# A new order of one step's instructions in a fused convolution, gelu and two-matrix kernel

## The chip, the cores and the metric

The kernel runs on one core of a Trainium2 chip. Its time is the device time of one execution in microseconds (us). A core has a matrix engine (TensorE, PE in the profile, with its weight loads listed as PEld), a vector engine (VectorE, DVE), an activation engine (ScalarE, ACT), a general engine (GpSimd, POOL) and an engine that here only issues transfers (SyncE, SP). Each engine works through its own instructions in the order in which they were written, and waits where one needs something that isn't there yet. SBUF is the memory on the chip that all engines read and write; PSUM is the small memory in eight banks that TensorE writes its products to.

## The reference

The input x is 8 sequences of 4096 rows of 192 values. Each of 8 heads (24 columns each) has 7 weights; after a softmax over the 7, every column is convolved along its sequence with its head's weights, looking back only:

```
w   = exp(weight - max) / (sum + 1e-9)                   # 8 x 7
out[b, s, h, :] = sum over k of w[h, k] * x_pad[b, s + k, h, :]      # 7 taps, 6 zeros in front
```

The result, as 32768 rows of 192, goes through two matrices with a gelu between them:

```
h = x @ w_in                          # 192 -> 2048
g = h * (1 / (1 + exp(-1.702 * h)))
return g @ w_out                      # 2048 -> 192
```

All of it is float32 (w_in and w_out come as float64 and are brought to float32 in the kernel's opening).

## The kernel before, in words

**Steps.** The rows are cut into 32 steps (`big` = 0 to 31); a step takes 512 rows from a sequence of the first four and the same 512 from its counterpart in the other four. Steps 0 and 1 have a prologue and a list of their own (`OPENING`) for their first products; steps 2 to 31 run through `first_products(big, ..., ORDER)`. Steps 1 to 31 then run `second(...)` with the list `PLAN`. Nothing is planned at run time or by a scheduler: `ORDER` and `PLAN` are lists written by hand, and the position of an item in its list is the position of its instructions on the engine that carries them out. Two items on different engines can change places in the list without a change to either engine's order; two items on one engine can't.

**First products, x @ w_in.** Both matrix products are done with fewer multiplications than the plain way, in the manner of Strassen: sums of blocks of the left matrix times sums of blocks of the right one, and the products added and subtracted into the results. For x @ w_in there are 20 block products (`TERMS`) for each half of the columns, so 40 in a step. A product is four matmul passes of 64 rows by 512 columns (L598 in the profile): two row halves of TensorE work side by side on two banks, and each matmul counts as two passes. A pair of passes, one for each row half, is the unit of the rhythm; a product has two pairs.

An item of `ORDER` has this form: the half that it belongs to (0, 1, or 2 for the next step's half 0), its kind and its operands. Operands whose name begins with `a` are pairs of PSUM banks, taken from a list of free ones at the first use and given back after the last one (so the order also decides which banks a product gets); those that begin with `k` are rooms in SBUF (`ROOM_OF` says which, and several names share one room).

- `(v, "prod", t, "aN")`: product t is added into aN (TensorE, L598).
- `(v, "copy", "kN", "aM", 1)`: ScalarE copies PSUM to a room (L633), or, with -1, negates in PSUM (L635). The copy of a product into a room is what later products of the other half, or of the same, are taken from.
- `(v, "sum", d, a, op, b)`: VectorE adds or subtracts (L639), each 128x512 half apart where a PSUM bank is in it.
- `(v, "gelu", b, u, src, sign)`: ScalarE's gelu of a finished block of h, written to `g` (L615 from PSUM, L620 from a room). Gelus k9 and k7 are those of the rooms with these names.
- `("tap",)`: ScalarE multiplies x of the step after next by one weight of the convolution (L483). `("add", n)`: POOL adds n such taps to the convolution's blocks `conv_t` (L501); the last columns' taps are added by accumulating DMAs instead (`tree`, L506).
- `("done",)`: what is left of the taps' additions for the next step, one more sum of blocks on POOL, and the crossing of that "open" block. `("begin",)` puts the next step's ten sums of blocks (`SUMS_C`) on a list, and every `("vsum",)` carries out one on POOL (L355 and L357, `conv_t<-conv_t`). `("cross",)` issues the two transfers on SP's queue that copy finished blocks to the other row half (L526), where the matmuls of that row half read them.
- `("turn", c)`: VectorE transposes one third of x (L438). `("turn", 2)` is the last reader of the buffer `xin`, and issues the loads of x for the step after (eight transfers on SP's queue, L78).
- `("g", i)`: entry i of `EARLY_G`, a sum of blocks of `g` that the second products need (VectorE, L355 and L357; blocks 0 and 1 are in `osbs`). Entry 0 makes block 6, entry 1 makes block 0 in `osbs`, entry 2 adds that block into block 8 by an accumulating DMA that POOL issues (L831, `g<-osbs`), entries 3 and 4 make block 1.

At the end of the first products of half 0 the items of half 1 are already mixed in, and at the end of half 1 the next step's product 0 and (in `final` of `PLAN`) its copy k8.

**Second products, g @ w_out.** `PLAN` has 25 products of 128 rows by 32 columns in four column tiles (L855): three of the tiles work on the "main" product, the fourth on a "side" product. `("main", f, s, to, first)` and `("side", f, s, to)` name them, and each `("go", n)` issues n groups of four column tiles; there are 78 groups. A finished side product is copied out of PSUM by ScalarE (L880). `("seed", d, s, sign)` is a copy on ScalarE that starts a bank or a room from another, `("join", d, a, op, b)` a sum of such values on VectorE (L357, 96x256), `("sum", d, a, op, b)` a sum of blocks of `g` on VectorE (L357, 128x1024), and `("acc", d, a)` one by an accumulating DMA of POOL's queue. `turn` and `store` transpose the result on VectorE and send it out on SP's queue; `tap`, `tree`, `vsum` and `cross` are those from above, for the steps to come.

**What follows what around the change.** In half 0, the room that the sum k0 reads (as k8) is the room that the copy k4 writes, and k4 frees bank a3 for product 14. Product 2 writes a3, product 6 writes a8, which k0 reads. At the end of half 1 stand the sums a7 and k7 on VectorE: the last product (before: 13) waits for a7, and the second products' banks come free with k7 and the copies and gelus after it. Product 19 of either half writes bank a4, which the negated copy a5 reads just before.

Of the kernel before, what the change touches and what calls it, by code (L numbers as in the profile page):

```python
# [15 lines left out]
def kernel(  # L16
# [80 lines left out]
    g = consts.tile([P, NG, 2, 2, NG, T], F32)  # L97
# [398 lines left out]
    tree, adds = [], []  # L496
# [144 lines left out]
    def plain(u, m, n, v, slot, ks=range(NC), first=0):  # L641
# [2 lines left out]
            product1(slot, NC * (2 * u + m) + k, 2 * k + n, 0, v, k == first)  # L644

    ORDER = [
        (0, "prod", 6, "a8"), (0, "sum", "k0", "a8", "-", "k8"), (0, "prod", 2, "a3"), (0, "copy", "k4", "a3", 1),
        (0, "prod", 12, "a2"), ("tap",), ("tap",), ("tap",), ("tap",), ("add", 4), (0, "prod", 16, "a0"),
# [4 lines left out]
        (0, "prod", 10, "a4"), ("turn", 1), (0, "gelu", 3, 1, "k3", 1), (0, "prod", 17, "a1"),  # L653
# [6 lines left out]
        ("turn", 2), (1, "copy", "k4", "a3", 1), (0, "gelu", 3, 0, "k9", 1), (1, "prod", 12, "a2"), ("done",),  # L660
        ("begin",), ("vsum",), (1, "prod", 16, "a0"), (1, "sum", "a1", "a2", "-", "k0"), (1, "prod", 14, "a3"),
        (1, "copy", "k1", "a0", 1), ("g", 0), (1, "prod", 9, "a2"), (1, "sum", "a4", "a2", "-", "k1"),
        (1, "prod", 3, "a1"), ("vsum",), ("vsum",), ("vsum",), ("vsum",), (1, "copy", "k2", "a1", 1),
        (1, "prod", 15, "a3"), (1, "prod", 7, "a4"), ("vsum",), (1, "prod", 1, "a1"),
# [3 lines left out]
        (1, "prod", 19, "a4"), (1, "prod", 11, "a1"), ("vsum",), (1, "prod", 8, "a5"),  # L668
        (1, "sum", "a6", "k6", "-", "a4"), (1, "prod", 5, "a4"), (1, "gelu", 0, 1, "a1", 1), ("g", 4),
        (2, "prod", 0, "a3"), (1, "gelu", 1, 0, "a5", 1), (1, "sum", "a7", "a4", "+", "k2"),  # L670
        (1, "gelu", 2, 1, "k5", 1), (1, "prod", 4, "a6"), (1, "prod", 13, "a4"), ("vsum",),
        (1, "sum", "k7", "a7", "-", "k6"), (1, "sum", "k9", "a4", "-", "k0"), (1, "gelu", 0, 0, "a6", 1),
        (1, "gelu", 2, 0, "k7", 1), ("cross",), (1, "gelu", 3, 0, "k9", 1), ("cross",), ("done",),
    ]
    SEED_AHEAD = ("copy", "k8", "a3", 1)
    ROOM_OF = ((4, 0, 3, 2, 1, 1, 0, 1, 1, 2), (0, 1, 4, 2, 3, 3, 2, 3, 3, 2))
# [97 lines left out]
    def store(big, n, o=None, queues=(nc.sync,) * 3):  # L774
# [13 lines left out]
        (6, 6, "-", 10), (0, 5, "+", 6), (8, 8, "+", 0), (1, 7, "-", 6), (1, 1, "-", 11),  # L788
    ]
    PLAN = [  # L790
        ("side", 13, 16, "k0"), ("main", 1, 5, "p2", 1), ("vsum",), ("go", 2), ("sum", 14, 14, "-", 18), ("go", 1),
        ("vsum",), ("vsum",), ("go", 1), ("main", 16, 10, "p3", 0), ("go", 1), ("tap",), ("go", 1), ("vsum",),
        ("go", 2), ("main", 0, 14, "p0", 1), ("go", 2), ("seed", "p4", "p2", 1), ("go", 1), ("seed", "k1", "p3", 1),
# [34 lines left out]
    def sum_g(dst, a, op, b=None):  # L828

        if op == "acc":  # L830
            nc.gpsimd.dma_start(out=spot(dst), in_=spot(a), accum_op=ALU.add)  # L831
        else:
            add_up(spot, dst, a, op, b)
# [3 lines left out]
    def second(big, bx, bs, by, final, last):  # L837
# [5 lines left out]
        side, count = [], [0]  # L843
# [47 lines left out]
        def out_store(n, o):  # L891
# [9 lines left out]
            sum=sum_g, acc=lambda d, a: sum_g(d, a, "acc"), main=begin_main, side=begin_side, go=go, seed=seed,  # L901
            join=lambda d, a, op, b: add_up(value, d, a, op, b), turn=out_turn, store=out_store,
            tap=next_tap, cross=cross_piece, final=final, vsum=next_sum, tree=add_taps,
        )
        for item in PLAN:
            ops[item[0]](*item[1:])
        assert not side and not now["steps"] and count[0] == NC * len(SIDE_HALF)
        while sums_left:
# [355 lines left out]
```

## Time and profile before

| | |
|---|---|
| median of 3 runs | 2262.8 us (2262.54 to 2262.89) |
| profiled execution | 2262.78 us, of which its span is 2261.1 us |
| PE busy | 2248.2 us, 99% |
| VectorE busy | 1985.3 us, 88% |
| ScalarE busy | 1707.7 us, 76% |
| POOL busy | 1063.9 us, 47% |
| PE, L598 (first products, steps from 1) | 5152 matmuls of 64x512 |
| transfers, mean over the span | 132 GB/s |
| q0, the queue that POOL's transfers run on | 150.69 MB, 37.0% of 16 engines' span |
| q1, the one that SP's run on | 142.99 MB, 27.8% |
| granted TensorE clock | 1.00 |

Busy time of PE is modelled from the starts, so 99% tells that it rarely has nothing in flight, not that it never loses time. In a row of the timeline stand, from left to right, the start in us from the span's beginning, the time from the first start to the last end, the engine, the line, the operation, what it writes and reads, the shape, and how many instructions of that kind the row holds; in square brackets stands the idle time of the engine ahead of the row and what ended it. A row with "x2" and two starts of one engine is two instructions, one behind the other. In the table of stretches a row has the stretch, its length, and for each engine (PE, PEld, DVE, ACT, POOL) the busy time and the number of instructions, then the granted clock, the share of time in which transfers ran, and GB/s. The steady step read in the prediction is step 16, whose first products begin at 1215.57 us, and whose second products run from 1250.98 to 1284.92 us.

### The profile page before, as it was taken

The page shows a single profiled execution, that of the slowest core. Times are in us where ns is not written, and L with a number is a line of the kernel's source. Part 1 is how long each engine was busy: PE and PEld are TensorE (multiplying, and loading weights), DVE is VectorE, ACT ScalarE, POOL GpSimd, SP SyncE. Part 2 cuts the span into 40 slices and gives each one's busy share as a digit, 9 for nine tenths or more (in the row PEclk, how much of TensorE's full clock was granted, in tenths as well). Part 3 has the DMA queues.
Part 4 walks back from the last instruction along what each step waited for, and adds up shares of the span by engine and source line. Part 5 has one row for each costly group of instructions (what it writes and reads, how often), then busy time and mean ns, then how long its engine had stood idle before and what let it go on. Part 6 is the DMA issues. An engine that isn't in the chain of part 4 may idle for free.

```text
span 2261.1 us, 62136 instructions
## 1 busy us (share of the span) xinstructions
PE 2248.2 (99%) x24966; PEld 1552.0 (69%) x24966; DVE 1985.3 (88%) x2970; ACT 1707.7 (76%) x3233; POOL 1063.9 (47%) x1098
## 2 busy tenths in 40 slices
PE   9999999999999999999999999999999999999999
PEld 5366567766777766777667776667776677766775
DVE  8998888988889888889888898888988888988888
ACT  8677877777777778777787777787777877777754
POOL 1545544455543555444555445554355544455510
PEclk9999999999999999999999999999999999999999
DMA  8986657766667666576565776666866657765543
GB/s 198 174 158 133 125 114 150 143 128 127 121 131 159 128 128 126 111 160 140 125 132 114 141 152 128 129 124 118 163 134 128 124 114 151 144 127 103 104 92 71
DMA packets 275679, 298.05 MB, mean 132 GB/s; under 512 B 119104, under 2 KB 203328, under 8 KB 275392
## 3 DMA queue, kind: packets, MB, share of 16 engines
q0 software_dynamic: 57648, 150.69, 37.0%
q1 hardware_dynamic: 216096, 142.99, 27.8%
q8 instruction: 198, 3.24, 0.6%
q14 instruction: 89, 0.73, 0.1%
q10 hardware_dynamic: 1648, 0.39, 0.1%
HBM read 53.15 MB, written 25.17 MB: 35 GB/s over the span
## 4 chain that ended last, share of the span: by engine, by line
PE 96%; DVE 2%; ACT 1%; issue 1%; DMA 1%; POOL 0%; DVEq 0%; ACTq 0%; POOLq 0%; SPq 0%
PE slot L598 49%; PE slot L855 45%; PE slot L1120 1%; DVE g L357 1%; DMA g<-osbs 0%; PE slot L1115 0%; DVE room L357 0%; ACT g L615 0%; PE slot L946 0%; DVE room L639 0%; ACT w_form L483 0%; DMA xin<-in_x_dram 0%; DVE slot L639 0%; DVE room L355 0%; DVE osbs L771 0%
## 5 line engine op out<-in xcount | busy, mean ns | idle before, releaser
L598 PE MATMUL slot<-conv_t,w_in_s 64*128 64x512 f32 x5152 | 1147.4, 594 | 3.3 <-ACT room L633 1.5
L598 PEld LDWEIGHTS slot<-conv_t,w_in_s 64*128 64x128 f32 x5152 | 663.3, 186 | 474.6 <-issue 312.1
L855 PE MATMUL slot<-g,w_form 128*32 128x256 f32 x9672 | 894.2, 379 | 0.7 <-DVE room L357 0.7
L855 PEld LDWEIGHTS slot<-g,w_form 128*32 128x32 f32 x9672 | 575.6, 110 | 128.9 <-DVE room L357 2.1
L501 POOL TENSOR_TENSOR conv_t<-conv_t,g 128x512 f32<-128x512 f32 x354 | 449.0, 1275 | 88.4 <-ACT g L483 65.4
L855 PE MATMUL slot<-g,w_out_s 128*32 128x256 f32 x5952 | 467.5, 379 | 1.3 <-DVE g L357 0.8
L357 DVE TENSOR_TENSOR g<-g 128x1024 f32<-128x1024 f32 x372 | 450.4, 1224 | 8.0 <-DMA g<-osbs 1.0
L880 ACT COPY room<-slot 32x256 f32<-32x256 f32 x651 | 237.2, 364 | 289.8 <-PE slot L855 281.5
L639 DVE TENSOR_TENSOR room<-slot,room 128x512 f32<-128x512 f32 x620 | 383.6, 679 | 67.8 <-PE slot L598 67.8
L633 ACT COPY room<-slot 128x512 f32<-128x512 f32 x620 | 337.7, 595 | 77.7 <-PE slot L598 61.7
L483 ACT ACTIVATE g<-xt,cw 128x512 f32<-128x512 f32 x534 | 353.9, 715 | 3.7
L620 ACT ACTIVATE g<-room 128x1024 f32<-128x1024 f32 x248 | 265.7, 1071 | 79.0 <-DVE room L639 49.3
L615 ACT ACTIVATE g<-slot 128x512 f32<-128x512 f32 x528 | 282.5, 610 | 51.9 <-PE slot L598 32.8
L831 POOL DMA_DIRECT2D g<-g x124 | 128.1, 1038 | 355.0 <-PE slot L855 330.8
L639 DVE TENSOR_TENSOR slot<-slot,room 128x512 f32<-128x512 f32 x372 | 239.7, 689 | 53.8 <-PE slot L598 52.2
L855 PEld LDWEIGHTS slot<-g,w_out_s 128*32 128x32 f32 x5952 | 239.7, 110 | 43.2 <-DVE room L639 23.3
L355 POOL TENSOR_TENSOR conv_t<-conv_t 128x256 f32<-128x256 f32 x210 | 179.3, 860 | 129.2 <-PE slot L598 119.6
L855 PE MATMUL slot<-osbs,w_form 128*32 128x256 f32 x2232 | 229.5, 379 | 0.0
L506 POOL DMA_DIRECT2D g<-g x120 | 105.9, 883 | 238.1 <-ACT g L483 99.4
L855 PEld LDWEIGHTS slot<-osbs,w_form 128*32 128x32 f32 x2232 | 132.5, 110 | 23.6
L639 DVE TENSOR_TENSOR slot<-room,slot 128x512 f32<-128x512 f32 x124 | 79.8, 687 | 41.8 <-PE slot L598 41.8
L855 PE MATMUL slot<-room,w_form 128*32 128x256 f32 x1488 | 112.9, 379 | 0.0
(166 smaller groups left out, 1662.6 us busy)
## 6 DMA issues: line engine op xcount, KB each, us to landing
g<-g POOLq DMA_DIRECT2D x124, 512.0 KB, 6.5
xin<-in_x_dram SPq DMA_DIRECT2D x240, 180.0 KB, 4.2
conv_t<-conv_t SPq DMA_DIRECT2D x186, 192.0 KB, 5.4
g<-g POOLq DMA_DIRECT2D x120, 256.0 KB, 5.4
conv_t<-conv_t SPq DMA_DIRECT2D x186, 128.0 KB, 2.9
out_dram<-osbs SPq DMA_DIRECT2D x186, 128.0 KB, 2.7
g<-room POOLq DMA_DIRECT2D x31, 512.0 KB, 5.1
conv_t<-g POOLq DMA_DIRECT2D x60, 256.0 KB, 5.4
```

Of the source, the lines that this page charges most:

```text
L355: eng.tensor_add(v(dst), v(a), v(b))
L357: eng.tensor_sub(v(dst), v(a), v(b))
L483: act.mul(home, conv_src(big, c, k), cw[:, c, k : k + 1])
L501: nc.gpsimd.tensor_add(dst, dst, home)
L598: nc.tensor.matmul(slot[h], w_in_s[halves[h], a, v * P : (v + 1) * P], src, start=first, stop=True, skip_group_check=True,)
L615: act.activation(dst[:, :, h, :], src[h].rearrange("p (o t) -> p o t", o=2), AF.Gelu_apprx_sigmoid, scale=float(sign),)
L620: act.activation(dst.rearrange("p o h t -> p h o t"), src.rearrange("p h (o t) -> p h o t", o=2), AF.Gelu_apprx_sigmoid, scale=float(sign),)
L633: act.copy(bank(dst, h), bank(src, h))
L639: op(*(bank(t, h) for t in (dst, a, b)))
L831: nc.gpsimd.dma_start(out=spot(dst), in_=spot(a), accum_op=ALU.add)
L855: nc.tensor.matmul(dst, w, t, start=first, stop=last, skip_group_check=True)
L880: act.copy(to, d)
```

## The change

Both lists get a new order. No product, sum, copy, gelu, tap or transfer is added or taken away in steps 2 to 31, and each has the same operands; only positions differ, and with them the order on each engine, and which pair of PSUM banks an `a` name gets.

In `ORDER` (steps 2 to 31):

- In half 0 product 2 stands before product 6, with the sum k0 behind product 6, and the copy k4 behind product 12.
- The first four additions of taps stand at the head of the list, the second four behind the taps, and the last four near the end of half 0; `turn` 1 and 2 stand earlier.
- In half 1 the gelu k9 of half 0 stands ahead of the copy k4. `done` and `begin` follow it.
- The early sums of `g` are issued as 0, 3, 1, 2, 4, the three in the middle right behind one another. The sums of blocks on POOL are spread anew, and one crossing stands earlier.
- At the end of half 1 the products stand as 5, 4, 0 of the next step, 13, where they stood as 5, 0 of the next step, 4, 13. The crossing that was last stands ahead of gelu k7. Copies and gelus of half 1 change places by one or two.

In `PLAN`, which now holds for steps 2 to 31 (step 1 keeps the old list under the name `PLAN_1`), TensorE's groups stand in the order in which they stood; seeds, joins, sums of `g`, turns, block sums and crossings stand earlier or later between them. Lines behind the new list are 38 further down: L855 becomes L893, L880 becomes L918.

The core of the diff, first the head of half 0, the seam of the halves and the early sums, then the end of half 1:

```
     ORDER = [
-        (0, "prod", 6, "a8"), (0, "sum", "k0", "a8", "-", "k8"), (0, "prod", 2, "a3"), (0, "copy", "k4", "a3", 1),
-        (0, "prod", 12, "a2"), ("tap",), ("tap",), ("tap",), ("tap",), ("add", 4), (0, "prod", 16, "a0"),
-        (0, "sum", "a1", "a2", "-", "k0"), ("add", 4), ("turn", 0), (0, "prod", 14, "a3"), (0, "copy", "k1", "a0", 1),
+        ("add", 4), (0, "prod", 2, "a3"), (0, "prod", 6, "a8"), (0, "sum", "k0", "a8", "-", "k8"),
+        (0, "prod", 12, "a2"), (0, "copy", "k4", "a3", 1), ("tap",), ("tap",), ("tap",), ("tap",), ("add", 4),
+        (0, "prod", 16, "a0"), (0, "sum", "a1", "a2", "-", "k0"), (0, "copy", "k1", "a0", 1), (0, "prod", 14, "a3"),
...
-        (0, "prod", 10, "a4"), ("turn", 1), (0, "gelu", 3, 1, "k3", 1), (0, "prod", 17, "a1"),
-        (0, "copy", "a5", "a4", -1), (0, "copy", "k6", "a2", 1), (0, "prod", 19, "a4"), (0, "prod", 11, "a1"),
+        (0, "prod", 10, "a4"), (0, "gelu", 3, 1, "k3", 1), (0, "copy", "a5", "a4", -1), (0, "prod", 17, "a1"),
+        (0, "copy", "k6", "a2", 1), ("turn", 1), (0, "gelu", 2, 1, "k5", 1), ("turn", 2), (0, "prod", 19, "a4"),
...
-        ("turn", 2), (1, "copy", "k4", "a3", 1), (0, "gelu", 3, 0, "k9", 1), (1, "prod", 12, "a2"), ("done",),
-        ("begin",), ("vsum",), (1, "prod", 16, "a0"), (1, "sum", "a1", "a2", "-", "k0"), (1, "prod", 14, "a3"),
+        (1, "prod", 12, "a2"), (1, "prod", 16, "a0"), (0, "gelu", 3, 0, "k9", 1), ("done",),
+        (1, "copy", "k4", "a3", 1), ("begin",), (1, "sum", "a1", "a2", "-", "k0"), (1, "prod", 14, "a3"),
...
-        (1, "sum", "k3", "a4", "+", "k4"), (1, "sum", "k5", "a1", "-", "k1"), ("g", 1), (1, "prod", 18, "a2"),
-        (1, "gelu", 1, 1, "a3", 1), ("g", 2), (1, "prod", 10, "a4"), (1, "gelu", 3, 1, "k3", 1), ("g", 3),
+        (1, "gelu", 1, 1, "a3", 1), (1, "sum", "k5", "a1", "-", "k1"), ("vsum",), ("g", 3), ("g", 1), ("g", 2),
+        (1, "prod", 18, "a2"), (1, "prod", 10, "a4"), ("cross",), (1, "gelu", 3, 1, "k3", 1),
...
-        (2, "prod", 0, "a3"), (1, "gelu", 1, 0, "a5", 1), (1, "sum", "a7", "a4", "+", "k2"),
-        (1, "gelu", 2, 1, "k5", 1), (1, "prod", 4, "a6"), (1, "prod", 13, "a4"), ("vsum",),
-        (1, "sum", "k7", "a7", "-", "k6"), (1, "sum", "k9", "a4", "-", "k0"), (1, "gelu", 0, 0, "a6", 1),
-        (1, "gelu", 2, 0, "k7", 1), ("cross",), (1, "gelu", 3, 0, "k9", 1), ("cross",), ("done",),
+        (1, "gelu", 2, 1, "k5", 1), ("g", 4), (1, "prod", 5, "a4"), (1, "prod", 4, "a6"), ("vsum",),
+        (1, "gelu", 0, 1, "a1", 1), (2, "prod", 0, "a3"), ("vsum",), (1, "gelu", 1, 0, "a5", 1), ("vsum",),
+        (1, "sum", "a7", "a4", "+", "k2"), (1, "prod", 13, "a4"), (1, "gelu", 0, 0, "a6", 1),
+        (1, "sum", "k7", "a7", "-", "k6"), (1, "sum", "k9", "a4", "-", "k0"), ("cross",), (1, "gelu", 2, 0, "k7", 1),
+        (1, "gelu", 3, 0, "k9", 1), ("done",),
     ]
```

From `PLAN`, the first sums, the place around main 9, and the end (the old list stays as `PLAN_1`):

```
     PLAN = [
+        ("main", 0, 14, "p0", 1), ("go", 1), ("seed", "p4", "p2", 1), ("go", 2), ("sum", 7, 8, "-", 7),
+        ("sum", 2, 9, "-", 0), ("seed", "k1", "p3", 1), ("sum", 8, 8, "-", 16), ("tap",), ("sum", 5, 11, "-", 19),
+        ("go", 1), ("seed", "p5", "k1", 1), ("side", 19, 1, "k1"), ("main", 18, 0, "p2", 0), ("sum", 11, 7, "+", 11),
...
+        ("main", 20, 0, "p1", 0), ("join", "k2", "k7", "-", "p4"), ("go", 1), ("join", "k2", "k2", "-", "p2"),
+        ("go", 1), ("side", 6, 13, "k8"), ("go", 1), ("sum", 15, 15, "-", 16), ("tap",), ("go", 1), ("tap",),
+        ("main", 9, 6, "p4", 0), ("go", 3), ("join", "k9", "p1", "+", "k5"), ("cross",),
...
+        ("main", 24, 19, "p5", 0), ("go", 1), ("join", "k1", "p3", "-", "k3"), ("go", 2), ("final",),
+        ("join", "k2", "p2", "-", "k4"), ("turn", 0, 0, 1, "k1"), ("store", 0, 1), ("vsum",), ("cross",), ("go", 1),
...
+    PLAN_1 = [
         ("main", 0, 14, "p0", 1), ("go", 2), ("seed", "p4", "p2", 1), ("go", 1), ("seed", "k1", "p3", 1),
         ("sum", 7, 8, "-", 7), ("sum", 8, 8, "-", 16), ("go", 1), ("sum", 5, 11, "-", 19), ("seed", "p5", "k1", 1),
...
-        for item in PLAN:
-        for item in PLAN:
+        for item in PLAN if big > 1 else PLAN_1:
             ops[item[0]](*item[1:])
```

More of the change, by code (lines that the diff above doesn't have):

```diff
@@ L650 @@
         (0, "prod", 9, "a2"), (0, "sum", "a4", "a2", "-", "k1"), (0, "prod", 3, "a1"), (0, "copy", "k2", "a1", 1),
[2 rows of a table removed]
-        (0, "prod", 10, "a4"), ("turn", 1), (0, "gelu", 3, 1, "k3", 1), (0, "prod", 17, "a1"),
[6 rows of a table removed]
-        ("turn", 2), (1, "copy", "k4", "a3", 1), (0, "gelu", 3, 0, "k9", 1), (1, "prod", 12, "a2"), ("done",),
-        ("begin",), ("vsum",), (1, "prod", 16, "a0"), (1, "sum", "a1", "a2", "-", "k0"), (1, "prod", 14, "a3"),
-        (1, "copy", "k1", "a0", 1), ("g", 0), (1, "prod", 9, "a2"), (1, "sum", "a4", "a2", "-", "k1"),
@@ L672 @@
-        (1, "sum", "k7", "a7", "-", "k6"), (1, "sum", "k9", "a4", "-", "k0"), (1, "gelu", 0, 0, "a6", 1),
-        (1, "gelu", 2, 0, "k7", 1), ("cross",), (1, "gelu", 3, 0, "k9", 1), ("cross",), ("done",),
+        ("turn", 0), (0, "prod", 15, "a3"), (0, "prod", 7, "a4"), (0, "prod", 1, "a1"), (0, "prod", 18, "a2"),
+        (0, "sum", "k3", "a4", "+", "k4"), (0, "sum", "k5", "a1", "-", "k1"), (0, "gelu", 1, 1, "a3", 1),
+        (0, "prod", 10, "a4"), (0, "gelu", 3, 1, "k3", 1), (0, "copy", "a5", "a4", -1), (0, "prod", 17, "a1"),
@@ L790 @@
     PLAN = [
[13 rows of a table added]
+        ("sum", 13, 18, "+", 4), ("sum", 6, 9, "-", 5), ("acc", 7, 10), ("acc", 18, 14), ("main", 2, 5, "p4", 0),
+        ("go", 1), ("tap",), ("go", 2), ("tap",), ("tap",), ("tree",), ("go", 1), ("acc", 12, 9),
[6 rows of a table added]
+        ("main", 10, 14, "p0", 0), ("tap",), ("tree",), ("go", 2), ("sum", 6, 6, "-", 17),
[13 rows of a table added]
+    ]
+    PLAN_1 = [
         ("side", 13, 16, "k0"), ("main", 1, 5, "p2", 1), ("vsum",), ("go", 2), ("sum", 14, 14, "-", 18), ("go", 1),
```

4 lines of the change are left out of this document (removed), and 40 rows, old and new, of tables (ORDER, PLAN).

## The prediction

> **What bounds the kernel now.** I read the page's busy times and its chain first, then two stretches of one steady step (its first products, its second products), then each engine's timeline in that step.
>
> ```profile
> span 2261.1 us, 62136 instructions
> PE 2248.2 (99%) x24966; PEld 1552.0 (69%) x24966; DVE 1985.3 (88%) x2970; ACT 1707.7 (76%) x3233; POOL 1063.9 (47%) x1098
> PE 96%; DVE 2%; ACT 1%; issue 1%; DMA 1%; POOL 0%; DVEq 0%; ACTq 0%; POOLq 0%; SPq 0%
> ```
> ```profile
> 1215.57:1250.98 35.41, 35.41 (x161) 20.68 (x160) 29.85 (x45) 28.68 (x50) 25.00 (x24) 1.00 0.55 114
> 1250.98:1284.92 33.94, 33.94 (x625) 29.06 (x624) 31.00 (x47) 24.81 (x52) 9.43 (x11) 1.00 0.79 154
> ```
> The chain is TensorE's for 96%, and one step is 35.41 + 33.94 = 69.35 us. Ends of matmuls are modelled, so "busy" says nothing of stalls; the starts do. The weight loads at the seam of the two phases show both rhythms:
>
> ```profile
> 1248.16 0.26 PEld L598 LDWEIGHTS slot<-conv_t,w_in_s 64*128 64x128 f32 x2 [0.17 <-issue]
> 1248.59 0.26 PEld L598 LDWEIGHTS slot<-conv_t,w_in_s 64*128 64x128 f32 x2 [0.17 <-issue]
> 1249.08 0.55 PEld L598 LDWEIGHTS slot<-conv_t,w_in_s 64*128 64x128 f32 x3 [0.24 <-issue]
> 1249.93 0.29 PEld L598 LDWEIGHTS slot<-conv_t,w_in_s 64*128 64x128 f32 x2 [0.30 <-DVE slot L639]
> 1250.98 0.15 PEld L855 LDWEIGHTS slot<-g,w_out_s 128*32 128x32 f32 x6 [0.76 <-DVE room L639]
> 1251.13 0.14 PEld L855 LDWEIGHTS slot<-g,w_form 128*32 128x32 f32 x2
> 1251.22 0.12 PEld L855 LDWEIGHTS slot<-g,w_out_s 128*32 128x32 f32 x3
> 1251.44 0.12 PEld L855 LDWEIGHTS slot<-g,w_out_s 128*32 128x32 f32 x3
> ```
> A pair of first-phase passes (both 64-row halves together) comes every 0.43 us (1248.16, 1248.59), a group of four column tiles every 0.22. With 80 pairs and 156 groups a step would be 80 x 0.43 + 156 x 0.216 = 68.1 us; some 1.3 us are left, and most of that is the changeover, where the other tile shape starts only when the last pair is nearly out (1249.93 to 1250.98). So a new order can win some 0.4 us a step in waits, while TensorE takes any new wait in full.
>
> **The waits of before that I count.** (a) At the end of the first products the last pair waits for the sum a7 on VectorE: 0.30 of idle before 1249.93 where other rows have 0.17, and its second pass is put off too. I take 0.16 (0.13 to 0.17). (b) The first group of the second products is 0.24 long (1250.98 to 1251.22) against 0.22: its side bank is still read by the sum k7. 0.03. (c) At the negated copy a5, product 19 waits until ScalarE has read the bank:
>
> ```profile
> 1226.23 1.07 ACT L635 ACTIVATE slot<-slot 128x512 f32<-128x512 f32 x2 [0.25 <-PE slot L598]
> 1226.88 0.29 PEld L598 LDWEIGHTS slot<-conv_t,w_in_s 64*128 64x128 f32 x2 [0.40 <-POOL conv_t L501]
> 1227.36 0.29 PEld L598 LDWEIGHTS slot<-conv_t,w_in_s 64*128 64x128 f32 x3 [0.18 <-ACT slot L635]
> 1227.85 0.23 PEld L598 LDWEIGHTS slot<-conv_t,w_in_s 64*128 64x128 f32 x2 [0.20 <-issue]
> 1228.28 0.23 PEld L598 LDWEIGHTS slot<-conv_t,w_in_s 64*128 64x128 f32 x2 [0.20 <-issue]
> ```
> The loads come 0.48 and 0.49 apart instead of 0.43, behind a start that is itself late: 0.11 to 0.20. The order of products 10, 17, 19 and of the copy is the same in the changed kernel, in both halves, so (c) stays and nothing is gained.
>
> **The change, part by part.** The number of instructions stays; positions move.
>
> 1. In half 0 product 2 now stands before product 6. The sum k0 needs product 6, and the copy k4 writes the room that k0 reads, so the path product 6, k0, k4, product 14 starts one product later.
>
> ```profile
> 1215.22 0.59 ACT L633 COPY room<-slot 128x512 f32<-128x512 f32 x1
> 1216.22 1.95 ACT L483 ACTIVATE g<-xt,cw 128x512 f32<-128x512 f32 x3
> 1218.20 1.07 ACT L633 COPY room<-slot 128x512 f32<-128x512 f32 x2
> 1217.16 1.25 DVE L639 TENSOR_TENSOR room<-slot,room 128x512 f32<-128x512 f32 x2
> 1216.96 0.19 PEld L598 LDWEIGHTS slot<-conv_t,w_in_s 64*128 64x128 f32 x2 [0.24 <-issue]
> 1218.84 1.75 PEld L598 LDWEIGHTS slot<-conv_t,w_in_s 64*128 64x128 f32 x9 [0.39 <-ACT room L633]
> L598 PE MATMUL slot<-conv_t,w_in_s x5152: 589/589/694, 13.5 to 2221.1; 64*128 64x512 f32 x199
> ```
> Before, k0 runs from 1217.16, and k4 from 1218.20, right behind three taps; its second half ends at 1219.27. After, k0 waits for the second product: that one's last pass starts at 1216.96 and lasts 0.59, so k0 runs from 1217.61 (0.06 for the signal) to 1218.86, and the second half of k4 from 1218.93 to 1219.52, 0.25 late. Product 14, the fifth, is due at 1215.57 + 4 x 0.86 + 0.1 = 1219.11. Its second half then starts at 1219.58; TensorE issues in order, so the second pass of its first half, due at 1219.54, comes 0.06 behind that, 0.10 late, and the next pair, as in (c), 0.04 to 0.09 more. I take 0.16, between 0 (all of it inside the halves' lag) and 0.30 (the lateness in full). Product 2 itself now waits for the copy k8, ScalarE's last of the step (1215.22 + 0.59 = 1215.81), which holds back one half by 0.3, within the lag that product 14 makes anyway: 0.
>
> 2. The early sums of g in half 1 stand as 3, 1, 2 instead of 1, 2, 3, where 2 is POOL's accumulate and needs sum 1.
>
> ```profile
> 1243.32 1.41 DVE L355 TENSOR_TENSOR osbs<-g 128x1024 f32<-128x1024 f32 x1
> 1244.65 1.21 DVE L357 TENSOR_TENSOR osbs<-g 128x1024 f32<-128x1024 f32 x1
> 1246.98 1.69 DVE L357 TENSOR_TENSOR osbs<-osbs,g 128x1024 f32<-128x1024 f32 x1
> 1248.59 1.28 DVE L639 TENSOR_TENSOR slot<-slot,room 128x512 f32<-128x512 f32 x2
> 1242.11 1.54 POOL L355 TENSOR_TENSOR conv_t<-conv_t 128x256 f32<-128x256 f32 x2
> 1245.27 0.87 POOL L831 DMA_DIRECT2D g<-osbs  x1 [1.63 <-ACT room L633]
> 1245.88 1.70 POOL L357 TENSOR_TENSOR conv_t<-conv_t 128x256 f32<-128x256 f32 x2
> 1247.65 1.60 POOL L355 TENSOR_TENSOR conv_t<-conv_t 128x256 f32<-128x256 f32 x1
> ```
> The accumulate now stands ahead of the block sum that ran until 1243.65, and waits for the second sum on VectorE instead of the first. So POOL computes nothing while these two run, and the first, 1.41 beside a POOL sum, should cost 1.21 like the second: 0.2 off VectorE's path to a7 (which is the row at 1248.59). That path starts from products 7 and 1; it moves 0.16 later with them and is 0.2 shorter, while the last pair is due 0.16 later. So (a) goes: -0.16. Behind the accumulate wait four block sums on POOL and their crossings on SP's queue, some 3 us later than before; their next reader is a product of the next step, 30 us on: 0.
>
> 3. The first four additions of taps move from behind the taps to the head of the list, where POOL waited:
>
> ```profile
> 1219.97 2.50 POOL L501 TENSOR_TENSOR conv_t<-conv_t,g 128x512 f32<-128x512 f32 x2 [2.18 <-ACT g L483]
> ```
> POOL gets through by about that much earlier, and so do the crossing that waits for it, and the loads of x behind that on SP's queue (the transpositions that free their buffer are earlier too). Gelu k9 goes before the copy k4 of half 1: one activation more ahead of a copy that was 0.7 us early: 0, but the nearest of these. The first second-phase group no longer shares a bank with k7: (b) goes, -0.03.
>
> 4. In the second products TensorE's order is the same; seeds, joins and sums of g change by a place or two.
>
> ```profile
> 1252.24 4.76 DVE L357 TENSOR_TENSOR g<-g 128x1024 f32<-128x1024 f32 x4
> 1269.25 0.41 DVE L357 TENSOR_TENSOR room<-room,slot 96x256 f32<-96x256 f32 x1
> g<-osbs POOLq DMA_DIRECT2D x30, 512.0 KB, 7.2
> ```
> VectorE goes from sum to sum (four in 4.76 us), so its places shift by at most one sum of 1.2. The tightest reader that I find is main 9, 44 groups of 0.432 in, at 1250.98 + 19.01 = 1269.99: the join before it ends at 1269.66, 0.33 ahead, and keeps its place: 0. The last crossing moves behind the first stores on SP's queue, with its reader (product 19) 10 us later: 0.
>
> The sum for a step: +0.16 - 0.16 - 0.03 = -0.03. Thirty steps use both lists: -0.9 us. The profiled execution took 2262.8 us (its span and 1.7 around it), which is the median of the runs as well: 2261.9, in round figures 2262.
>
> **Rivals.**
> - A, slower: POOL's block sums, which stood apart, now lie all behind the accumulate and beside the last early sum of g (1246.98), and a7 comes late. That row's 1.69 holds 0.48 of waiting beside 1.21; if a whole block sum (1.54 / 2 = 0.77) falls on it, a7 is 0.29 later. With +0.16 for the shift and -0.2 for the first sum, a7 ends 0.25 later than before, and the step is 0.25 - 0.03 = 0.22 longer: 2269.4. It decides as soon as the row at 1246.98 is over 1.9. The Trainium skill ("SBUF — State Buffer", section "SBUF: two separate sides") has the mechanism: a VectorE operation with two SBUF inputs and a GpSimd one that reads SBUF take the shared port as a whole, and the loser waits out the other's instruction. By that rule 0.77 is the most that can be lost there, and the 1.41 and 1.69 agree with it; in which order the two meet, no row of before tells.
> - B, slower: the accumulate is issued at 1245.9 instead of 1245.27, and the sum that reads its result is the second of the four at 1252.24, due at 1253.4: 7.5 us, and 0.33 more before main 9 waits. The median landing is 7.2; at 8.2, with the crossings that now start behind it in its way, each step loses 0.4: 2275. Against it: the loads of x are out of the way sooner.
> - C, faster: part 1 costs nothing and (a) and (b) go, -0.19 a step: 2257. For it: before, a late half of the same product (0.39 of idle at 1218.84) cost the other half nothing. Against: then it was 0.25 less late.
> - The relief of 2 doesn't come, and (a) stays: 0.16 - 0.03 a step, 2266.7, still within the bound below.
>
> **How the numbers follow.** Within 0.2% (4.5 us, about what a measurement of this kernel can tell from no change), 2258.3 to 2267.3, lie my forecast and the last rival: 0.37. C and whatever wins more (up to 0.4 a step): 0.22. A, B and waits that I have not seen, for which a full TensorE has no cover: 0.41, of it A 0.14 and B 0.13. The range leaves out 0.1 on either side: from 2255.5, C with 0.05 a step more, to 2274, just short of B at its full price. The forecast's own range is 2259 to 2267.
>
> **What would show it.** Part 1: k4 ends 0.25 later, and 0.48 stands once where 0.43 was before product 14's second pass. Part 2: both early sums at 1.21, and no wait for VectorE before the last pair. Part 3: 0.22 for the first second-phase group. Part 4: second products of 33.9 us still. If these take over 34.1, B or a VectorE wait that I took for covered is the cause; first products under 35.2 or over 35.6 would mean that parts 1 and 2 are mis-sized.

## The result, and the profile after

The changed kernel takes 2269.07 us (median of 10 runs, 2267.05 to 2271.05) against 2262.85 us (10 runs, 2262.27 to 2263.92): a ratio of 1.0027, with a 95% interval of 1.0017 to 1.0036. The forecast was 2262.0, the range 2255.5 to 2274.0; so the kernel became slower by 6.2 us, just over the prediction's bound of 0.2% and with an interval clear of 1, where no change was thought likeliest. The runs also lie further apart than before, 4 us instead of under 2.

The page of the changed kernel, profiled in an execution of 2267.96 us:

```profile
span 2266.3 us, 62042 instructions
PE 2251.1 (99%) x24966; PEld 1392.0 (61%) x24966; DVE 1997.7 (88%) x2970; ACT 1715.0 (76%) x3233; POOL 1062.0 (47%) x1098
PE 97%; DVE 1%; ACT 1%; issue 0%; DMA 0%; ACTq 0%; SPq 0%; DVEq 0%
```

The same step 16 (counted by `big` it is 17) in the table of stretches, its first products and then its second ones:

```profile
1217.37:1253.05 35.68, 35.68 (x164) 23.22 (x160) 30.13 (x45) 28.93 (x50) 24.99 (x24) 1.00 0.58 118
1253.05:1286.86 33.81, 33.81 (x625) 20.18 (x625) 31.16 (x46) 24.81 (x52) 9.43 (x11) 1.00 0.77 151
```

First products take 0.27 more than before (35.41), second ones 0.13 less (33.94): a steady step is 0.13 to 0.14 longer, and 29 of them make 3.9 of the 5.2 us between the two profiled executions. The rest is one long step (below), 1.2 us over its like, where the kernel before had one of 0.7 (36.09, also from 521.32); an end that is 1.7 us longer; and 0.9 won in the first two steps' second products, beside small ones.

The seam of the two phases, on TensorE's weight loads:

```profile
1250.92 0.19 PEld L598 LDWEIGHTS slot<-conv_t,w_in_s 64*128 64x128 f32 x1 [0.24 <-issue]
1251.40 0.29 PEld L598 LDWEIGHTS slot<-conv_t,w_in_s 64*128 64x128 f32 x2 [0.30 <-DVE slot L639]
1252.00 0.29 PEld L598 LDWEIGHTS slot<-conv_t,w_in_s 64*128 64x128 f32 x2 [0.30 <-DVE slot L639]
1253.05 0.12 PEld L893 LDWEIGHTS slot<-g,w_out_s 128*32 128x32 f32 x3 [0.76 <-issue]
1253.07 0.11 PEld L893 LDWEIGHTS slot<-g,w_form 128*32 128x32 f32 x1
1253.29 0.12 PEld L893 LDWEIGHTS slot<-g,w_out_s 128*32 128x32 f32 x3
```

Wait (a) is not gone: there are now two waits of 0.30 for VectorE (L639, the sum a7) where one stood before, and the loads come 0.48 and 0.60 apart. The side tile, though, loads 0.02 behind the main ones (1253.07), where before it came 0.15 behind (1250.98, 1251.13).

VectorE ahead of that, and POOL beside it:

```profile
1245.12 1.22 DVE L357 TENSOR_TENSOR osbs<-g 128x1024 f32<-128x1024 f32 x1
1246.25 1.22 DVE L355 TENSOR_TENSOR osbs<-g 128x1024 f32<-128x1024 f32 x1
1248.58 2.16 DVE L357 TENSOR_TENSOR osbs<-osbs,g 128x1024 f32<-128x1024 f32 x1
1250.66 1.28 DVE L639 TENSOR_TENSOR slot<-slot,room 128x512 f32<-128x512 f32 x2
```
```profile
1248.02 0.87 POOL L869 DMA_DIRECT2D g<-osbs  x1 [3.35 <-PE slot L598]
1248.63 1.02 POOL L355 TENSOR_TENSOR conv_t<-conv_t 128x256 f32<-128x256 f32 x1
1249.72 2.29 POOL L357 TENSOR_TENSOR conv_t<-conv_t 128x256 f32<-128x256 f32 x2
```

The first early sum of g is at 1.22, as forecast (1.41 before). But the last one takes 2.16 instead of 1.69. It starts while POOL's issue of the accumulate still runs (1248.02 to 1248.89) and the first block sum stands right behind; it ends 1.1 after that block sum does (1249.65), which is about its own 1.22. POOL's next sum then waits in turn. The sum a7 behind it starts 33.29 into the step where it started 33.02 in, 0.27 later.

The kernel before has the same loss once, in its own long step, which is 0.7 longer than the others. VectorE's last early sum there, and POOL's block sums beside it:

```profile
552.73 2.36 DVE L357 TENSOR_TENSOR osbs<-osbs,g 128x1024 f32<-128x1024 f32 x1
...
552.30 1.70 POOL L357 TENSOR_TENSOR conv_t<-conv_t 128x256 f32<-128x256 f32 x2
```

The long step, whose first products take 36.85 (from 521.32), on VectorE and POOL, and then the same place in step 16:

```profile
522.26 2.22 DVE L355 TENSOR_TENSOR room<-room 96x256 f32<-96x256 f32 x1
...
522.03 0.86 POOL L506 DMA_DIRECT2D conv_t<-g  x1 [2.97 <-DMA g<-g]
522.59 4.37 POOL L501 TENSOR_TENSOR conv_t<-conv_t,g 128x512 f32<-128x512 f32 x3
```
```profile
1218.32 0.38 DVE L355 TENSOR_TENSOR room<-room 96x256 f32<-96x256 f32 x1
...
1219.16 0.86 POOL L506 DMA_DIRECT2D conv_t<-g  x1 [3.02 <-DMA g<-g]
1219.72 2.93 POOL L501 TENSOR_TENSOR conv_t<-conv_t,g 128x512 f32<-128x512 f32 x2
```

It is the last join of the step before, a sum of 0.38. Where POOL issues its transfer 0.71 after the step's start, with the additions of taps (now at the head of the list) right behind it, the join takes 2.22; where it does so at 1.79, 0.38. The sum k0, the copy k4 and product 14 stand behind that join.

### The profile page after: what moved, and what is told of

The parts are those of the page before. It is cut to its first block, busy times and chain, and to the rows that moved or that the text cites. A ratio compares the mean times of both kernels' runs of the same rounds, so it can differ in the third digit from the quotient of the medians.

```text
span 2266.3 us, 62042 instructions
## 1 busy us (share of the span) xinstructions
PE 2251.1 (99%) x24966; PEld 1392.0 (61%) x24966; DVE 1997.7 (88%) x2970; ACT 1715.0 (76%) x3233; POOL 1062.0 (47%) x1098
## 4 chain that ended last, share of the span: by engine, by line
PE 97%; DVE 1%; ACT 1%; issue 0%; DMA 0%; ACTq 0%; SPq 0%; DVEq 0%
PE slot L598 50%; PE slot L893 45%; PE slot L1158 1%; DVE g L357 0%; PE slot L1153 0%; DVE room L357 0%; ACT g L615 0%; DVE room L355 0%; DMA xin<-in_x_dram 0%; ACT w_form L483 0%; DVE room L639 0%; DVE osbs L771 0%; ACTq L782 0%; ACT conv_t L998 0%; DVE xt L438 0%
## 5 line engine op out<-in xcount | busy, mean ns | idle before, releaser
L598 PEld LDWEIGHTS slot<-conv_t,w_in_s 64*128 64x128 f32 x5152 | 743.1, 186 | 403.3 <-issue 67.5
L893 PE MATMUL slot<-g,w_form 128*32 128x256 f32 x9672 | 894.6, 379 | 0.4 <-DVE room L357 0.3
L893 PEld LDWEIGHTS slot<-g,w_form 128*32 128x32 f32 x9672 | 484.3, 110 | 161.8 <-DVE room L357 1.4
L893 PE MATMUL slot<-g,w_out_s 128*32 128x256 f32 x5952 | 467.5, 379 | 1.3 <-DVE g L357 0.8
L501 POOL TENSOR_TENSOR conv_t<-conv_t,g 128x512 f32<-128x512 f32 x354 | 457.1, 1302 | 18.6
L918 ACT COPY room<-slot 32x256 f32<-32x256 f32 x651 | 237.5, 365 | 286.9 <-PE slot L893 277.5
L639 DVE TENSOR_TENSOR room<-slot,room 128x512 f32<-128x512 f32 x620 | 384.5, 682 | 59.8 <-PE slot L598 59.8
L633 ACT COPY room<-slot 128x512 f32<-128x512 f32 x620 | 342.5, 591 | 93.2 <-PE slot L598 70.7
L893 PEld LDWEIGHTS slot<-g,w_out_s 128*32 128x32 f32 x5952 | 241.6, 110 | 188.2 <-issue 22.0
L620 ACT ACTIVATE g<-room 128x1024 f32<-128x1024 f32 x248 | 260.8, 1066 | 105.1 <-DVE room L639 104.7
L639 DVE TENSOR_TENSOR slot<-slot,room 128x512 f32<-128x512 f32 x372 | 240.8, 692 | 83.7 <-ACT g L615 41.6
L355 POOL TENSOR_TENSOR conv_t<-conv_t 128x256 f32<-128x256 f32 x210 | 162.6, 780 | 142.3 <-PE slot L598 135.0
L893 PE MATMUL slot<-osbs,w_form 128*32 128x256 f32 x2232 | 225.6, 379 | 0.0
L893 PEld LDWEIGHTS slot<-osbs,w_form 128*32 128x32 f32 x2232 | 118.2, 110 | 41.7
L357 POOL TENSOR_TENSOR conv_t<-conv_t 128x256 f32<-128x256 f32 x120 | 111.8, 943 | 18.4 <-PE slot L598 12.4
L893 PE MATMUL slot<-room,w_form 128*32 128x256 f32 x1488 | 112.7, 379 | 0.0
```

Of the source, the lines that this page charges most:

```text
L355: eng.tensor_add(v(dst), v(a), v(b))
L357: eng.tensor_sub(v(dst), v(a), v(b))
L501: nc.gpsimd.tensor_add(dst, dst, home)
L598: nc.tensor.matmul(slot[h], w_in_s[halves[h], a, v * P : (v + 1) * P], src, start=first, stop=True, skip_group_check=True,)
L620: act.activation(dst.rearrange("p o h t -> p h o t"), src.rearrange("p h (o t) -> p h o t", o=2), AF.Gelu_apprx_sigmoid, scale=float(sign),)
L633: act.copy(bank(dst, h), bank(src, h))
```

## The experiments

The theories: S, POOL's block sums beside the last early sum of g make a7 late (the prediction's rival A); L, the halves' lag after the swap of products 2 and 6 (its part 1); H, the additions at the head shut VectorE out when they come early, which makes the long steps (first products of 36 us and more).

**Without the four block sums behind the accumulate.**

```
-        (1, "prod", 17, "a1"), ("vsum",), (1, "prod", 19, "a4"), ...
+        (1, "prod", 17, "a1"), ("skip",), (1, "prod", 19, "a4"), ...
```
(and likewise the three others; "skip" takes the sum off the list without carrying it out.)

> The changed kernel without the four block sums that POOL runs behind the accumulate (left out in steps 2 to 31, so the blocks 11 to 14 of the convolution keep older values). Theory S (these sums stretch the third early sum of g, and so a7): the third early sum takes 1.21 us instead of 2.16, a7 ends about 0.9 earlier, the last pair of first products waits no more, and the first products take 35.25 to 35.45 instead of 35.68; some 2256 to 2261 in all. Rival L (the halves' lag: product 2 waits for the copy k8, half 1 starts 0.33 behind, and stays behind): the third sum may be shorter, but the first products stay at 35.6 to 35.7, and the time at 2268.

Measured: 2269.5 in one run. A step without disturbance, its first products and the last early sum:

```profile
1079.08:1114.42 35.34, 35.34 (x164) 23.81 (x160) 29.69 (x46) 29.26 (x51) 21.26 (x20) 1.00 0.63 132
...
1110.27 1.22 DVE L357 TENSOR_TENSOR osbs<-osbs,g 128x1024 f32<-128x1024 f32 x1
```

S holds, as to the place and the size: 1.22, and 0.34 off the step. The whole didn't follow, because 12 of 29 steps were long ones, of 36.2 to 36.9, all with a join of 1.5 to 2.3. With less to do, POOL was sooner at the additions. That brought up H.

**The block sums late in the second products.** The four, and the one at the head of `PLAN`, behind the fourth accumulating transfer of taps:

```
-        ("tree",), ("tap",), ("go", 1), ("join", "k7", "k7", "+", "k3"), ("tree",), ("go", 1),
+        ("tree",), ("vsum",), ("vsum",), ("vsum",), ("vsum",), ("vsum",), ("tap",), ("go", 1), ...
```

> The changed kernel with these four block sums, and the one that stood at the head of PLAN, moved late into the second products (behind the fourth of the accumulating transfers of taps), and no work left out. Theory S: first products of 35.25 to 35.45, as without the sums; second products of 33.8 if VectorE's small joins there bear the company of POOL, up to 34.1 if not; so 2255 to 2261, or up to 2267 with the loss. Rival L: 2268.

Measured: 2388.23 (5 runs), 1.0558 [1.0543, 1.0572]. Neither theory: second products stay at 33.81, but first ones take 37.4 to 41.4. The weight loads early in a step, and SP's queue:

```profile
1281.06 0.42 PEld L598 LDWEIGHTS slot<-conv_t,w_in_s 64*128 64x128 f32 x4 [3.31 <-POOL conv_t L501]
...
1274.93 1.87 SPq L782 DMA_DIRECT2D out_dram<-osbs  x3
1276.90 1.23 SPq L526 DMA_DIRECT2D conv_t<-conv_t  x2
```

The sixth block sum (block 11) is the last of the group 9 to 11, which crosses together; so that crossing went out at 1276.90, behind stores, and TensorE stood 3.3 us at product 16, the fourth of the step and a reader of block 9. The edit was too coarse to say anything of S.

**Product 6 first again.**

```
-        ("add", 4), (0, "prod", 2, "a3"), (0, "prod", 6, "a8"), (0, "sum", "k0", "a8", "-", "k8"),
+        ("add", 4), (0, "prod", 6, "a8"), (0, "sum", "k0", "a8", "-", "k8"), (0, "prod", 2, "a3"),
```

> The changed kernel with product 6 ahead of product 2 in half 0 again (part 1 undone). Theory S: both halves start together as before, but up to product 14 no earlier; products 7 and 1 and with them a7 come at the same time or 0.13 later: a step of 69.5 to 69.65, 2268 to 2273. Rival L, and part 1 of the prediction (+0.16 a step for the swap): the step is 0.16 to 0.33 shorter, 2258 to 2264.

Measured: 2268.78 (10 runs), 1.0021 [1.0012, 1.003]; steady steps of 35.68 and 33.81, as in the change, with three long steps in the profiled execution. The swap neither costs nor brings anything while a7 is late.

**The old `PLAN` in the last step.**

```
-        for item in PLAN if big > 1 else PLAN_1:
+        for item in PLAN if 1 < big < N_BIG - 1 else PLAN_1:
```

> The changed kernel with the old PLAN in the last step alone. From the last start of the second products' groups on, the changed kernel needs 1.7 us more to its end, with a store's issue of 2.1 us on ScalarE's queue ahead of its last copy. If the new order of the last joins, turns and stores makes this: 1.7 less, 2266 to 2268 against 2268 to 2270. If it is chance or the transfers' state: no change.

Measured: 2269.0 (8 runs), 1.0025 [1.0015, 1.0035]. No change; from the last start of a matmul to the end it takes 7.5 us (7.6 in the change, 5.95 in the kernel before), and among the kernels below that have the new `PLAN` at the end, 5.8 to 7.65. So the order of the last joins and stores doesn't set it; what does stays open.

**The additions of taps back behind the taps.**

```
-        ("add", 4), (0, "prod", 2, "a3"), ...
-        ... ("tap",), ("tap",), ("tap",), ("tap",), ("add", 4),
+        (0, "prod", 2, "a3"), ...
+        ... ("tap",), ("tap",), ("tap",), ("tap",), ("add", 4), ("add", 4),
```

> The changed kernel with the first four additions of taps behind the taps again, where POOL waits for ScalarE (the head of part 3 undone). In the changed kernel's trace one step's first products took 36.85 us instead of 35.68, where POOL's first addition began at 1.27 in the step, ahead of VectorE's last join, which took 2.2 us instead of 0.4; without the block sums 12 steps of 30 were such. Theory H (the additions at the head shut VectorE out whenever the accumulating transfer ahead of them lands early): no such step is left, steady steps stay at 35.68 + 33.81, the runs lie closer together than 4 us, and the median is 1 to 3 us lower, 2266 to 2268. Rival (these steps come from somewhere else, as the one of 36.09 in the kernel before does): they stay, 2269.

Measured: 2265.97 (11 runs, 2264.84 to 2267.25), 1.0012 [1.0003, 1.002]: 3.1 us less than the change, and runs within 2.4. No long step in the profile. A step (from 868.02) in which the transfer is issued as early as 0.62:

```profile
868.64 0.86 POOL L506 DMA_DIRECT2D conv_t<-g  x1 [2.93 <-DMA g<-g]
872.65 2.49 POOL L501 TENSOR_TENSOR conv_t<-conv_t,g 128x512 f32<-128x512 f32 x2 [3.15 <-DMA conv_t<-conv_t]
...
868.96 0.38 DVE L355 TENSOR_TENSOR room<-room 96x256 f32<-96x256 f32 x1
```

The join takes 0.38 with the issue beside it, since no addition follows. H holds as to the long steps. How much of the 3.1 us they are isn't shown here: of the 2.9 between the two profiled executions, the step from 521 makes 1.5, the end 1.0 and the opening 0.4.

**And the early sums apart from the block sums.** On top of the last:

```
-        ... (1, "sum", "a4", "a2", "-", "k1"), ("vsum",), (1, "prod", 15, "a3"),
+        ... (1, "sum", "a4", "a2", "-", "k1"), ("g", 3), ("vsum",), (1, "prod", 15, "a3"),
-        ... ("vsum",), ("g", 3), ("g", 1), ("g", 2),
+        ... ("vsum",), ("g", 1), ("g", 2), ("g", 4),
-        (1, "gelu", 2, 1, "k5", 1), ("g", 4), (1, "prod", 5, "a4"), ...
+        (1, "gelu", 2, 1, "k5", 1), (1, "prod", 5, "a4"), ...
```

> As the last, and the early sums of g moved away from the block sums that stretch them: the sum of block 1 with 7 and 6 stands behind the sum a4 of half 1, where VectorE had 1.2 us idle, and the other one of block 1 behind the accumulate, so that none is left between a6 and a7. No work is left out. Theory S: a7 is in time, first products of 35.3 to 35.45, second of 33.8, no odd steps: 2255 to 2260. If the moved sum stretches beside POOL's sums and makes k3 and k5 late: 35.5 to 35.9, 2262 to 2272. Rival L (the halves' lag): 35.68 whatever VectorE does at the end, 2266 to 2268.

Measured: 2257.53 (11 runs), 0.9976 [0.9967, 0.9985]: faster than the change, and 5.7 us below the kernel before. Step 16:

```profile
1211.76:1247.11 35.35, 35.35 (x165) 23.08 (x161) 29.96 (x46) 29.23 (x51) 26.07 (x24) 1.00 0.55 119
```

**`ORDER` alone, `PLAN` alone.** `for item in PLAN_1` in all steps; and the old `ORDER` with the new `PLAN`.

> The new ORDER with the old PLAN in all steps. Theory S: all of what the steady step lost is ORDER's: first products of 35.68. The second products went from 33.94 to 33.81 because their last products give their banks back sooner; if that is PLAN's doing, they are at 33.94 here, and some 2272 in all; if it is ORDER's, 33.81 and 2269.

> The old ORDER with the new PLAN in steps 2 to 31. Theory S: first products of 35.4 as before, since the sixth block sum stands ahead of the accumulate. If PLAN makes the second products shorter, they are at 33.81, and the whole takes 2257 to 2259; if ORDER does, 33.94 and 2261 to 2263.

Measured: 2265.34 and 2264.79, one run each. The table of stretches of step 16, `ORDER` alone and then `PLAN` alone:

```profile
1215.62:1251.30 35.68, 35.68 (x164) 23.15 (x160) 30.13 (x45) 28.91 (x50) 25.01 (x24) 1.00 0.53 108
1251.30:1285.11 33.81, 33.81 (x625) 20.17 (x624) 31.02 (x46) 24.78 (x52) 9.43 (x11) 1.00 0.81 158
```
```profile
1217.54:1252.95 35.41, 35.41 (x161) 20.76 (x161) 29.86 (x45) 28.71 (x50) 25.02 (x24) 1.00 0.58 121
1252.95:1286.89 33.94, 33.94 (x625) 28.69 (x624) 31.17 (x47) 24.83 (x52) 9.43 (x11) 1.00 0.75 145
```

Both shifts of the steady step, the loss and the gain, are `ORDER`'s. `PLAN` moves nothing there. I had expected 2269 for `ORDER` alone; its profiled execution has no long step, and POOL's transfer is issued no sooner than 0.78 into a step. For `PLAN` alone I had expected 2263 at most; some of its steps' first products take 35.5 to 36.1, and why stays open.

**Product 6 first, with the sums apart.** The swap of the third experiment in the fast version.

> The version with the sums apart, and product 6 ahead of product 2 again: part 1 by itself, with no late a7 to hide it. Part 1 of the prediction: the swap costs 0.16 a step, so first products of 35.19 and 2252 to 2254. Rival L2 (product 2's wait for the copy k8 sets half 1 back by 0.33 at the start, where it would have waited 0.3 at product 14 anyway): the same within 0.1 a step, 35.3 to 35.45, 2256 to 2261.

Measured: 2257.52 (10 runs), 0.9977 [0.9967, 0.9986]; first products:

```profile
1212.42:1247.80 35.38, 35.38 (x164) 19.68 (x160) 30.41 (x46) 29.06 (x51) 25.18 (x24) 1.00 0.58 120
```

0.03 more than with product 2 first, and the same time. L falls.

**Order or number.** Three kernels with the additions back behind the taps: the early sums in the old order 1, 2, 3; six block sums instead of five ahead of the accumulate, as before the change; and both.

```
-        ... ("vsum",), ("g", 3), ("g", 1), ("g", 2),
+        ... ("vsum",), ("g", 1), ("g", 2), ("g", 3),
```
```
-        ... ("vsum",), ("g", 3), ("g", 1), ("g", 2),
+        ... ("vsum",), ("vsum",), ("g", 3), ("g", 1), ("g", 2),
-        ... (1, "prod", 17, "a1"), ("vsum",), (1, "prod", 19, "a4"),
+        ... (1, "prod", 17, "a1"), (1, "prod", 19, "a4"),
```

> The changed kernel with the additions back behind the taps, and the early sums of g in the old order 1, 2, 3, with five block sums ahead of the accumulate and four behind it as in the change. Theory S: the accumulate goes out 1.2 us earlier and so do the block sums behind it, so fewer of them lie beside the last early sum: that one at 1.7 to 2.0, a7 0.2 to 0.45 earlier than in the change, first products of 35.35 to 35.5. If the number behind the accumulate (four for three) makes the loss: 2.16 and 35.68 still.

> As the last, but with the change's order 3, 1, 2, and six block sums ahead of the accumulate, as in the kernel before. If the number is what counts: the first early sum at 1.41, the last one at 1.69, first products of 35.35 to 35.5. If it is the place of the accumulate: 2.0 to 2.2 for the last, with 1.41 for the first, so a7 0.1 to 0.2 later than in the change: 35.7 to 35.9.

> Both at once: order 1, 2, 3 and six ahead, so part 2 undone as a whole. Theory S: 1.41, 1.21 and 1.69 as in the kernel before, a7 0.27 earlier than in the change, first products of 35.35 to 35.45, second of 33.81. If it stays at 35.68, the loss is not part 2's.

Measured: 2257.79, 2292.75 and 2263.45, one run each. The old order (stretch, last early sum, POOL):

```profile
1211.52:1246.87 35.35, 35.35 (x165) 23.16 (x161) 29.70 (x46) 29.23 (x51) 26.30 (x24) 1.00 0.56 119
...
1242.73 1.22 DVE L357 TENSOR_TENSOR osbs<-osbs,g 128x1024 f32<-128x1024 f32 x1
...
1241.03 0.87 POOL L869 DMA_DIRECT2D g<-osbs  x1 [2.20 <-PE slot L598]
1241.64 1.02 POOL L355 TENSOR_TENSOR conv_t<-conv_t 128x256 f32<-128x256 f32 x1
1242.74 2.49 POOL L357 TENSOR_TENSOR conv_t<-conv_t 128x256 f32<-128x256 f32 x2
```

Six ahead, in the change's order:

```profile
1229.55:1266.14 36.59, 36.21 (x165) 23.18 (x161) 31.05 (x45) 28.91 (x50) 26.08 (x24) 1.00 0.60 126
...
1260.99 2.83 DVE L357 TENSOR_TENSOR osbs<-osbs,g 128x1024 f32<-128x1024 f32 x1
...
1260.42 0.87 POOL L869 DMA_DIRECT2D g<-osbs  x1 [2.76 <-ACT room L633]
1261.03 1.71 POOL L357 TENSOR_TENSOR conv_t<-conv_t 128x256 f32<-128x256 f32 x2
```

Both, where the last early sum is that of the kernel before:

```profile
1215.97:1251.43 35.46, 35.46 (x165) 23.19 (x161) 29.91 (x45) 28.91 (x50) 26.09 (x24) 1.00 0.57 121
...
1247.41 1.70 DVE L357 TENSOR_TENSOR osbs<-osbs,g 128x1024 f32<-128x1024 f32 x1
```

The order decides, since it sets when the accumulate goes out and which of POOL's sums meets VectorE's. With the old order VectorE's sum begins at 1242.73, 0.01 ahead of POOL's second block sum; it runs at its own 1.22, and POOL's two sums take 2.49 (its others take 0.73 each). I had expected 1.7 to 2.0 there. With the change's order the accumulate goes out 1.1 later, and VectorE's sum meets the block sum that stands right behind it; that one is recorded 0.05 later than VectorE's (1248.63 against 1248.58) and goes first all the same. With six ahead two block sums stand back to back there (1.71 for both), VectorE gets in only after the second, and loses 2.83 - 1.22 = 1.61; I had expected first products of 35.9 at most.

The run with six ahead and the change's order has one step with the other outcome: in the one from 526.40 the accumulate is issued 0.10 behind the start of VectorE's sum (557.94 against 557.84); the sum takes 1.21, and the first products 35.35. And in three steps of the run with the old order VectorE's sum begins 0.04 to 0.11 behind the second block sum instead of ahead of it: then POOL goes first, and VectorE's sum takes 1.70 to 1.77.

**The old order of the early sums alone,** with the additions still at the head; and the kernel with both moved back, again.

> The changed kernel with the early sums of g in the old order 1, 2, 3 and nothing else; the additions of taps stay at the head. Theory S and H together: first products of 35.35 as with the additions moved back, but steps that are 0.8 to 1.4 us longer come back wherever POOL's first addition begins ahead of VectorE's last join: 3 to 13 of 30, 2260 to 2273, and runs that lie further apart. If the order 3, 1, 2 brought the long steps too (by sending the accumulate, and what stands behind it, 1.1 us later): none, 2256 to 2259.

> The old order 1, 2, 3 with the additions back behind the taps, which had one run (2257.79), timed: 2256 to 2259 if that run stands, whatever the long steps come from.

Measured: 2274.11 (5 runs), 1.0051 [1.0039, 1.0064]; and 2257.63 (10 runs), 0.9978 [0.9968, 0.9987]. In the first, 16 of 29 steps are long, one of them:

```profile
592.23:628.91 36.68, 35.98 (x165) 25.93 (x161) 31.26 (x46) 29.49 (x51) 25.27 (x24) 1.00 0.56 119
...
593.17 2.05 DVE L355 TENSOR_TENSOR room<-room 96x256 f32<-96x256 f32 x1
...
592.77 0.86 POOL L506 DMA_DIRECT2D conv_t<-g  x1 [2.94 <-DMA g<-g]
593.34 1.59 POOL L501 TENSOR_TENSOR conv_t<-conv_t,g 128x512 f32<-128x512 f32 x1
```

The others are at 35.35. So the two causes are apart: the late accumulate costs 0.33 in a steady step, and the additions at the head cost 0.7 to 1.7 in some, in more of them the sooner POOL gets there. In the five traces with long steps (the change, and the first, third, fourth and this experiment) every step in which POOL's transfer is issued up to 0.76 after its start has a stretched join, and none in which it is issued from 0.80 on.

## Why the prediction was wrong

- **What bounds the kernel:** right. TensorE is in the chain for 97%, and each new wait shows in full.
- **Part 1 (the swap, +0.16): wrong in its sum.** Copy k4 does end later, at 1220.12 + 1.18 = 1221.30, 3.93 into the step where it was 3.70: 0.23 for the 0.25 forecast.

```profile
1220.12 1.18 ACT L633 COPY room<-slot 128x512 f32<-128x512 f32 x2
```

  But the wait of product 2 for the copy k8, priced at 0, and the one at product 14 are the same lag counted at two places. By the starts of its matmuls half 1 now begins 0.33 behind half 0 (0.01 before), and then loses 0.10 at product 14 where it lost 0.32. Measured alone, the swap is -0.03 a step (35.35 against 35.38), a little below the lower bound of 0.
- **Part 2 (early sums, -0.16): the step that failed.** The first half was right (1.41 to 1.22). The second, that the accumulate's later issue costs nothing because the block sums' readers are 30 us away, looked at who waits for POOL and not at whom POOL holds up. Rival A named it, at the place and nearly at the size: "decides as soon as the row at 1246.98 is over 1.9" (2.16), and a7 0.25 later (0.27 by the rows, counted from the step's start). It had a chance of 0.14; the row that should have weighed more was its own, 1.69 for a sum that takes 1.21 elsewhere, which says that POOL already won the race there. And the trace of before had a row for the order in which the two meet: the 2.36 of its long step. Against the old order in the same kernel the cost is 35.68 - 35.35 = 0.33 a step. Its total, 2269.4, is near the measured one by other terms: a steady step is 0.13 longer and not 0.22, and the long steps and the end make up the rest.
- **The rule from the Trainium skill ("SBUF — State Buffer", section "SBUF: two separate sides").** That the loser waits out the other's whole instruction agrees with the runs (2.16, which ends 1.1 after POOL's sum). That the first to start wins agrees with them where no transfer of POOL's stands right in front (1242.73 against 1242.74); by the recorded starts it doesn't where one does (1248.58 against 1248.63, and VectorE lost). My use of it, 0.77 at most, didn't hold: 2.16 - 1.22 = 0.94 was lost to the end of an issue and one sum, and 1.61 to two sums with no gap between them.
- **Part 3 (additions at the head, 0): wrong.** I named who is served earlier and not what stands beside the additions at the new place. Moving them back is worth 3.1 us (2269.07 to 2265.97).
- **(b), -0.03: right in kind, mis-sized.** It measured -0.13 (33.94 to 33.81). Before, the side tile loaded 0.15 behind the main tiles and stayed so to the last group: its last matmul starts 33.63 into the phase and theirs at 33.49, where in the change they start at 33.50 and 33.49. So the delay of one tile at the start of the phase is paid at its end in full, and not by the first group's 0.24 against 0.22.
- **Part 4 (0): right.** With `PLAN` alone the second products are at 33.94, as before. Rival B didn't come: the accumulate's median landing is 4.8 us here (7.2 before).
- **The last rival ("(a) stays", 2266.7)** and C were off for the same reason: (a) got worse. The fast versions do come to C's 2257 and its -0.19 a step, but by other sizes: 0.06 in the first products and 0.13 in the second, for the 0.16 and 0.03 of the prediction.

The range held the time; the likeliest case was the wrong one.

## What to carry to other kernels

When an engine off the critical path is let loose earlier or later, ask what the others do at that moment, and not only who waits for its results: VectorE and POOL exclude each other here when both add in SBUF (1.22 for a sum alone, 1.7 to 2.83 where POOL went first), and an edit that shifts one by a microsecond decides who is first in nearly every step. A row that is longer than its like (1.69 beside 1.21) is a race already being lost, and the first place to look when anything around it moves. And a wait counted at two places of the same half is one lag: follow one half from start to end before adding.

## What I had not expected of the hardware

VectorE's sum can lose to more than one of POOL's instructions: where two block sums stood back to back right behind the accumulate it waited out both (2.83 for 1.22, and 2.36 in the kernel before), while after a gap of some 80 ns between them it got in (in the change after the first of them, 1249.65 to 1249.72). The gap isn't the whole of it: in the three steps with the old order above it got in between two block sums that stand just as close. What decides there stays open.

A recorded start isn't always the moment that counts, either. VectorE's was ahead of POOL's by 0.05 in the change, by 0.04 with six ahead and by up to 0.38 at the join (recorded at 0.94 into the step, with the addition at up to 1.32), and it lost each time to a sum that stood right behind a transfer issued by POOL. At the join the bound is sharp: with the transfer issued at 0.76 or sooner after the step's start the join of 0.38 took 1.4 to 2.3, at 0.78 (`ORDER` alone) or later 0.38. An issue without an addition behind it, at 0.62, held nothing up. What of the issue makes POOL first isn't shown.
